# A new hand-written order for a fused sliding-window attention and gMLP kernel, with output stores as steps of their own

## The chip, the cores and the metric

One NeuronCore of a Trainium2 chip runs the whole computation. The metric is device time of one execution in microseconds, median over runs; smaller is better. TensorE is called PE in the profile's rows (PEld is its weight load), VectorE DVE, ScalarE ACT, GpSimd POOL and SyncE SP.

## What is computed

From one input x (2048 tokens by 512, bf16), normalised once, two branches are added to x: causal attention over a window of 256 keys with 32 heads of 16, and a gMLP whose spatial weight mixes all 2048 tokens.

```python
xn = _layernorm(x, axis=-1)
return x + _A_ref(xn, A_wqkv, A_wo) + _B_ref(xn, B_w_in, B_w_sp, B_b_sp, B_w_out)

# _A_ref: q, k, v from x @ wqkv, 32 heads of 16
mask = (idx[:, None] - idx[None, :] >= 0) & (idx[:, None] - idx[None, :] < W)   # W = 256
p = _softmax(jnp.where(mask[None, None], q @ k.T * Dh ** (-0.5), -1000000000.0), axis=-1)
out_A = (p @ v) @ wo

# _B_ref: F = 1376, Fh = 688
z = _gelu(x @ w_in)
z1 = z[..., :Fh].copy()
z2 = _layernorm(z[..., Fh:], axis=-1)
g = jnp.einsum('ts,bsf->btf', w_sp, z2) + b_sp[None, :, None]
out_B = (z1 * g) @ w_out
```

## The kernel before

The work is cut into small steps, each a Python function of a few instructions, and the order of all steps is written out by hand as three strings, STAGE1, STAGE2 and STAGE3 (lines 68 to 169), which `run` (L597) reads token by token. A token is a letter and its arguments. Every engine executes its instructions in the order in which they are emitted, so the strings set the order on each engine and on each DMA queue; semaphores only delay. A DMA that is issued on SP or POOL holds up the issues behind it in the same queue until what it waits for is there.

Tokens are split in 16 tiles of 128 (n below). The steps that the text speaks of:

- Stage 1, normalisation and the gMLP's first half. `a,n` takes statistics of x tile n on VectorE (L260), `A,lo,hi` makes 1/std of tiles lo to hi-1 on POOL in two instructions (L222), `b,n` normalises a tile on VectorE (L265; six buffers), `B,n` only centres tiles 0 to 2. `t`/`T` transpose a tile on TensorE and copy it, `d,n` transposes it by a DMA on SP (L297). `z,n,half,bank,p0,p1` multiplies a tile by half of w_in in two pairs of chunks (L304), `y,n,half,bank` applies gelu on ScalarE (L317). Of the second half `c,n` takes statistics on VectorE (L324), `C,lo,hi` makes 1/std on POOL, `e,n` normalises in place on VectorE (L330). `I,i` are set-up steps (L603): I,12 to I,19 load the attention's output weight, I,20 and I,21 the gMLP's, all as DMAs on POOL; I,8 clears regions on VectorE, I,9 one on POOL.
- Projections. For head group G (four of eight heads) and token block j (four of 512 tokens), `Q,G,j,bank,c0,c1` and `K,...` multiply chunks c0 to c1-1 into one of two PSUM banks, v or w (L337); `q,G,j,bank,engine` and `k,...` evict the bank on VectorE (D) or ScalarE (A) into a staging tile with two buffers; `F,G,j` and `G,G,j` spread it to its place by four to six, and four, DMAs of up to 64 KB (L357, L381), on SP for G = 0 and on POOL otherwise. `P,n`/`p,n` do the same for the values, without a spread.
- Attention. The window is laid out as a band of 4864 columns per head group, in ten pieces g. `S,G,g,e` (L425) writes 128 x 2048 scores into the only score tile, four PSUM banks; `X,G,g,e` (L436) is the exponential on ScalarE that empties it. So scores and exponentials alternate, 76 of each. `M,k` masks on VectorE, `V,i` (L489) multiplies by the values, `N,i,part` (L505) transposes and divides on VectorE.
- Mixing. `w,n` loads the transposed rows n of w_sp by a DMA on SP into one of three buffers (L530), `H,n,half,bank,c0,c1` multiplies chunks of it into bank v or w (L535), `h,n,half,bank` adds the bias and gates on VectorE. `u,n` transposes the result by a DMA on SP (L550); u,n overwrites what u,n-1 read.
- Output. `r,n` loads x tile n again by a DMA on POOL (L558) into one of two buffers, `O,n,bank,...` and `R,n,bank,...` multiply by the gMLP's and the attention's output weight into one bank, `o,n,bank` (L577) adds x on VectorE into one of two buffers and stores it by a DMA on SP.

Stage 2 runs attention, mixing and the first output tiles together; stage 3 has the last output tiles, for which four more PSUM banks (i, j, k, l) are free. The pool of the w_sp buffers is opened after stage 1's pools are closed (L684), and so may take their place.

Of the kernel before, what the change touches and what calls it, by code (L numbers as in the profile page):

```python
# [90 lines left out]
P,0,w,0,4 p,5,v,D M,0 S,0,1,1 I,13 P,1,v,0,4 p,0,w,D X,0,1,1 p,1,v,D P,2,w,0,4 M,1 P,11,v,0,1
w,1 p,2,w,A S,0,2,0 I,14 c,12 P,11,v,1,3 X,0,2,0 P,3,w,0,3 e,10 C,12,16 P,11,v,3,4 M,2 F,0,2 V,0
e,5 p,11,v,A S,0,2,1 I,15 e,15 P,3,w,3,4 X,0,2,1 P,8,v,0,4 p,3,w,D P,10,w,0,4 p,8,v,D G,0,2 M,3
Q,0,3,v,0,1 p,10,w,A S,0,3,0 I,16 e,6 Q,0,3,v,1,2 X,0,3,0 P,13,w,0,4 e,2 e,8 Q,0,3,v,2,3 e,14
V,1 M,4 p,13,w,A S,0,3,1 I,17 Q,0,3,v,3,4 X,0,3,1 P,12,w,0,4 q,0,3,v,D e,12 F,0,3 P,15,v,0,4
p,12,w,D p,15,v,A M,5 S,0,4,0 I,18 Q,1,0,w,0,1 X,0,4,0 P,4,v,0,4 w,2 Q,1,0,w,1,4 p,4,v,D N,0,0
q,1,0,w,A S,0,4,1 I,19 K,1,0,v,0,2 X,0,4,1 F,1,0 N,0,1 H,0,0,w,0,3 K,1,0,v,2,4 e,9 V,2 k,1,0,v,D
S,0,5,0 I,20 M,6 H,0,0,w,3,7 G,1,0 X,0,5,0 P,14,v,0,1 N,1,0 H,0,0,w,7,8 P,14,v,1,2 H,0,0,w,8,12
e,13 P,14,v,2,3 H,0,0,w,12,13 M,7 S,0,5,1 I,21 H,0,0,w,13,16 X,0,5,1 V,3 h,0,0,w N,1,1
H,0,1,w,0,5 M,8 S,0,6,0 H,0,1,w,5,9 X,0,6,0 M,9 P,14,v,3,4 H,0,1,w,9,16 p,14,v,D H,1,0,v,0,2  # L100
h,0,1,w S,0,6,1 N,2,0 H,1,0,v,2,3 u,0 K,1,1,w,0,1 X,0,6,1 H,1,0,v,3,5 K,1,1,w,1,2 H,1,0,v,5,6
K,1,1,w,2,4 w,3 k,1,1,w,D V,4 S,0,7,0 N,2,1 H,1,0,v,6,10 X,0,7,0 Q,1,1,w,0,1 M,10 H,1,0,v,10,16
Q,1,1,w,1,3 h,1,0,v S,0,7,1 M,11 Q,1,1,w,3,4 X,0,7,1 H,1,1,v,0,13 N,3,0 q,1,1,w,D M,12 S,0,8,0
F,1,1 H,1,1,v,13,16 X,0,8,0 H,2,0,w,0,11 h,1,1,v w,4 N,3,1 G,1,1 S,0,8,1 V,5 X,0,8,1 N,4,0
H,2,0,w,11,16 H,2,1,v,0,4 h,2,0,w S,0,9,0 M,13 H,2,1,v,4,6 X,0,9,0 Q,1,2,w,0,2 M,14 H,2,1,v,6,8
Q,1,2,w,2,3 N,4,1 H,2,1,v,8,9 V,6 S,1,0,0 Q,1,2,w,3,4 X,1,0,0 H,2,1,v,9,16 q,1,2,w,D H,3,0,w,0,6
h,2,1,v w,5 N,5,0 S,1,0,1 K,1,2,v,0,1 X,1,0,1 H,3,0,w,6,7 M,15 K,1,2,v,1,2 H,3,0,w,7,8
K,1,2,v,2,4 u,1 H,3,0,w,8,9 k,1,2,v,D V,7 M,0 S,1,1,0 H,3,0,w,9,16 X,1,1,0 N,5,1 H,3,1,v,0,7
# [613 lines left out]
```

## Time and profile before

| what | value |
|---|---|
| median of three runs | 266.68 us |
| the three runs | 264.35, 266.68, 269.54 us |
| the profiled execution, own time | 267.68 us |
| its span, first to last instruction | 266.0 us |
| granted TensorE clock, mean | 0.992 |
| busy TensorE, VectorE, ScalarE, POOL | 252.3, 187.1, 178.5, 90.1 us |
| 76 exponentials: busy, one | 142.6, 1.877 us |
| first and last exponential start | 49.91, 248.04 us |
| POOL's key copies: issue, landing (median) | 0.625, 4.5 us |
| SP's loads of w_sp: landing (median) | 5.2 us |

The profile is of one execution. A row of the timeline gives start, duration, engine and line, what is written from what, and in brackets how long the engine idled before and what ended that. A q behind an engine's name marks its queue of issues, where a duration can cover several issues (xcount). A row of windows gives a stretch, its length, and the busy time of each engine in it. TensorE's matmuls overlap, so that its busy time is an upper bound of its work.

### The profile page before, as it was taken

How to read it: one execution, taken by the hardware profiler on the slowest of the kernel's cores; microseconds unless marked ns; L12 is line 12 of the kernel's file. 1: busy time of each engine (PE TensorE's matmuls, PEld its weight loads, DVE VectorE, ACT ScalarE, POOL GpSimd, SP SyncE). 2: the span in 40 equal slices, each digit the busy share in tenths (PEclk: the TensorE clock that was granted, in tenths of full speed). 3: DMA queues.
4: the chain of work that ended last, by engine and by line, in shares of the span. 5: the costliest groups of instructions: out<-in, count | busy, mean ns of one | idle time of the engine just before them, and what ended most of it. 6: DMA issues, size and time to landing. Idle time of an engine off the chain costs nothing.

```text
span 266.0 us, 8993 instructions
## 1 busy us (share of the span) xinstructions
PE 252.3 (95%) x3876; PEld 140.4 (53%) x3916; DVE 187.1 (70%) x415; ACT 178.5 (67%) x137; POOL 90.1 (34%) x168
## 2 busy tenths in 40 slices
PE   7999999898999999999999979999989999999993
PEld 6565555343455566555555644565646544444541
DVE  4779977979688858476878654777467577666573
ACT  3675556788976867877778755867867786767300
POOL 6432230406080250197221923062163206511130
PEclk9999999999999999999999997999999999999999
DMA  6994243267474566779643872996396313422233
GB/s 196 364 266 99 55 93 70 49 142 172 78 174 125 100 141 111 99 175 212 123 91 79 167 127 62 108 148 121 74 172 130 70 32 111 131 81 83 81 98 99
DMA packets 69431, 32.65 MB, mean 123 GB/s; under 512 B 60288, under 2 KB 66528, under 8 KB 69392
## 3 DMA queue, kind: packets, MB, share of 16 engines
q1 hardware_dynamic: 64864, 22.50, 41.3%
q0 software_dynamic: 4496, 9.58, 15.4%
q8 instruction: 30, 0.49, 0.8%
q14 instruction: 9, 0.07, 0.1%
q10 hardware_dynamic: 32, 0.00, 0.0%
HBM read 8.41 MB, written 2.10 MB: 40 GB/s over the span
## 4 chain that ended last, share of the span: by engine, by line
PE 47%; DMA 13%; DVE 13%; issue 13%; POOL 8%; ACT 3%; SPq 1%; POOLq 0%; DVEq 0%; ACTq 0%
PE w L538 25%; PE w L339 7%; PE sS L429 6%; PE oP L501 5%; DMA x_ch<-in_A_x_dram 5%; DVE st L327 5%; PE w L394 3%; POOL q L366 3%; DMA wspT<-in_B_w_sp_dram 3%; DMA xs<-in_A_x_dram 2%; ACT E L443 2%; POOL kbd L387 2%; DMA kbd<-kz 2%; DVE st L262 2%; DVE xn L267 2%
## 5 line engine op out<-in xcount | busy, mean ns | idle before, releaser
L443 ACT ACTIVATE E<-sS 128x2048 bf16<-128x2048 f32 x76 | 142.6, 1877 | 50.7 <-PE sS L429 48.4
L538 PE MATMUL w<-z,wspT 128*128 128x344 bf16 x512 | 93.9, 314 | 1.9 <-DMA wspT<-in_B_w_sp_dram 1.1
L538 PEld LDWEIGHTS <-wspT 128*128 128x128 bf16 x512 | 47.1, 99 | 32.2 <-issue 5.6
L366 POOL DMA_DIRECT2D q<-qs x54 | 28.0, 527 | 73.5 <-DVE qs L355 36.8
L452 DVE TENSOR_TENSOR E<-E,mask 128x1024 bf16<-128x1024 bf16 x52 | 34.5, 672 | 4.8 <-ACT E L443 4.6
L339 PE MATMUL w<-xnT,wqkv 128*128 128x512 bf16 x105 | 34.8, 382 | 1.6 <-DVE v_all L405 0.8
L387 POOL DMA_DIRECT2D kbd<-kz x48 | 29.5, 625 | 13.6 <-DVE kz L379 8.9
L429 PE MATMUL sS<-q,kbd 32*128 32x320 bf16 (+4 forms) x816 | 30.5, 244 | 2.2 <-DMA kbd<-kz 1.8
L545 DVE SCALAR_TENSOR_TENSOR z1u<-w,b_all,z1u 128x344 bf16<-128x344 f32 x32 | 17.9, 560 | 17.7 <-PE w L538 17.6
L509 DVE STREAM_TRANSPOSE a<-oP 128x512 f32<-128x512 f32 x32 | 22.6, 705 | 9.2 <-PE oP L501 9.1
L501 PEld LDWEIGHTS <-v_all 64*17 64x17 bf16 x1920 | 22.3, 85 | 9.2 <-issue 9.0
L501 PE MATMUL oP<-E,v_all 64*17 64x256 bf16 (+3 forms) x1920 | 26.2, 230 | 0.0
L429 PEld LDWEIGHTS <-kbd 32*128 32x128 bf16 x816 | 12.5, 92 | 24.3 <-issue 22.6
L309 PEld LDWEIGHTS <-xnT 128*128 128x128 bf16 x208 | 18.1, 98 | 12.4
L560 POOL DMA_DIRECT2D x_ch<-in_A_x_dram x16 | 8.7, 545 | 38.4 <-DVE out_sb L579 32.7
L566 PE MATMUL w<-w_out_sb,z1u 128*128 128x512 bf16 x67 | 18.5, 381 | 0.6 <-DVE out_sb L579 0.4
L339 PEld LDWEIGHTS <-wqkv 128*128 128x128 bf16 x128 | 12.2, 98 | 12.2 <-issue 3.4
L394 PE MATMUL w<-wqkv,xnT 128*128 128x512 bf16 x61 | 15.7, 379 | 0.8 <-DVE v_all L405 0.3
L379 DVE CAST kz<-w 128x256 bf16<-128x256 f32 x28 | 10.5, 418 | 6.6 <-PE w L339 6.4
L522 DVE STREAM_TRANSPOSE oT<-b 128x256 bf16<-128x256 bf16 x32 | 14.2, 445 | 1.1
L327 DVE BATCH_NORM_STATS2 st<-z 128x6 f32<-128x344 bf16 x32 | 14.5, 496 | 0.0
L262 DVE BATCH_NORM_STATS2 st<-xs 128x6 f32<-128x512 bf16 x16 | 10.8, 677 | 4.6 <-DMA xs<-in_A_x_dram 4.6
(87 smaller groups left out, 246.4 us busy)
## 6 DMA issues: line engine op xcount, KB each, us to landing
kbd<-kz POOLq DMA_DIRECT2D x48, 64.0 KB, 4.5
q<-qs POOLq DMA_DIRECT2D x36, 64.0 KB, 3.0
x_ch<-in_A_x_dram POOLq DMA_DIRECT2D x16, 128.0 KB, 3.3
out_dram<-out_sb SPq DMA_DIRECT2D x16, 128.0 KB, 2.0
wqkv<-in_A_wqkv_dram SPq DMA_DIRECT2D x1, 1536.0 KB, 10.8
xs<-in_A_x_dram SPq DMA_DIRECT2D x2, 512.0 KB, 7.5
kbd<-kz SPq DMA_DIRECT2D x16, 64.0 KB, 2.1
q<-qs SPq DMA_DIRECT2D x14, 64.0 KB, 2.0
```

The source lines that it names most:

```text
L327: nc.vector.bn_stats(out=st[:, j, :], in_=z2[:, n, j * FQ : (j + 1) * FQ])
L339: nc.tensor.matmul(banks[bank], lhsT=wqkv[:, c, col : col + P], rhs=xnT[:, c, tok : tok + 512], start=(c == 0), stop=(c == NDC - 1),)
L366: eng.dma_start(out=q2[h : P : 2, e, c : c + w], in_=t[64 * e : 64 * e + 64, src0 + at : src0 + at + w],)
L387: eng.dma_start(out=kbd[h : P : 2, slot : slot + 4, e, :], in_=t[64 * e : 64 * e + 64, h, :].rearrange("p (k m) -> p k m", k=4),)
L394: nc.tensor.matmul(banks[bank], lhsT=xnT[:, c, n * P : (n + 1) * P], rhs=wqkv[:, c, 2 * D : 3 * D], start=(c == 0), stop=(c == NDC - 1),)
L429: nc.tensor.matmul(s_bank(s)[:, off + o : off + o + w], lhsT=kbd[32 * s : 32 * s + 32, slot, ee, :], rhs=q2[32 * s : 32 * s + 32, ee, c : ...
L443: nc.scalar.activation(out=dst, in_=src, func=ACT.Exp, scale=SM_SCALE)
L452: nc.vector.tensor_tensor(out=reg, in0=reg, in1=mask[:].rearrange("p a m -> p (a m)").unsqueeze(1).to_broadcast([P, 8, 128]), op=ALU.mult,)
L501: nc.tensor.matmul(skip_group_check=True, **args)
L509: nc.vector.transpose(out=a32[:].rearrange("p e c r -> p (e c r)"), in_=oP[i % 2][:])
L538: nc.tensor.matmul(banks[bank][:, 0:FQ], lhsT=w[:, c, :], rhs=z2[:, c, half * FQ : (half + 1) * FQ], start=(c == 0), stop=(c == NB - 1),)
L566: nc.tensor.matmul(banks[bank], lhsT=uT[:, c, :], rhs=w_out_sb[:, c, :], start=(c == 0), stop=False)
```

## The change

The three strings are written anew: nearly every step of the three stages changes place, the split of projections and mixing into chunks changes, and so do some banks and some evicting engines. The steps themselves and their number stay, with three differences. The output store is cut out of `o` and becomes a step `v,n`. The pool of the w_sp buffers is opened ahead of stage 1's pools, so that it has room of its own, and w,0 moves into stage 1. All loads of output weights (I,12 to I,21) move into the end of stage 1; before they stood in stage 2.

The diff, cut to the code and to the lines of the strings that the text speaks of:

```diff
 STAGE1 = """
...
-y,2,0,a z,4,1,b,0,2 b,2 y,3,0,o A,6,9 a,9 d,2 z,3,1,a,0,1 y,4,1,b z,5,1,o,0,2 b,6 A,9,10 a,10
-d,6 z,4,0,b,0,2 y,5,1,o b,7 A,10,11 b,8 d,7 a,11 z,5,0,o,0,2 y,4,0,b a,12 d,8 z,3,1,a,1,2
...
-z,6,1,b,0,2 c,3 d,10 z,7,1,o,0,1 y,6,1,b a,14 K,0,0,w,2,3 z,7,1,o,1,2 c,5 A,11,15 z,8,0,a,0,1
-y,7,1,o z,8,1,b,0,1 q,0,0,v,A b,11 z,9,1,o,0,2 b,12 d,11 b,13 c,6 z,8,1,b,1,2 d,13 K,0,0,w,3,4
...
-z,11,0,b,0,2 c,4 d,15 z,11,1,a,0,2 y,11,0,b c,0 F,0,0 z,14,0,b,0,2 y,11,1,a C,0,4 y,7,0,o C,4,8
-z,13,1,a,0,1 e,1 y,14,0,b c,9 G,0,0 K,0,1,v,3,4 z,12,1,o,0,1 z,13,1,a,1,2 c,8 z,12,1,o,1,2
...
-y,15,0,o c,13 z,10,0,b,0,1 y,14,1,a c,10 z,6,0,o,0,1 z,10,0,b,1,2 e,0 C,8,12 c,15 z,13,0,a,0,2
-y,10,0,b c,14 z,6,0,o,1,2 y,13,0,a z,12,0,b,0,2 y,6,0,o e,7 P,6,w,0,1 y,12,0,b
...
+b,0 y,2,0,b z,3,0,a,0,2 b,1 d,0 T,4,v,A a,7 y,2,1,o t,5,w z,3,1,b,0,2 a,8 d,1 T,5,w,A b,2 A,6,9
+z,4,0,o,0,2 y,3,1,b d,2 b,6 y,3,0,a z,5,0,b,0,1 b,7 d,6 y,4,0,o b,8 z,4,1,a,0,1 a,9 z,5,0,b,1,2
...
+b,10 a,12 K,0,0,w,3,4 d,10 y,6,0,a z,7,0,b,0,2 a,13 z,6,1,o,1,2 y,7,0,b a,14 z,8,1,a,0,1 y,6,1,o
+z,8,0,b,0,1 A,11,15 k,0,0,w,A z,8,1,a,1,2 b,11 z,8,0,b,1,2 y,8,1,a a,15 z,10,1,o,0,1 K,0,1,w,0,1
+b,12 z,7,1,a,0,2 c,2 d,12 z,10,1,o,1,2 y,7,1,a c,0 d,11 Q,0,0,v,3,4 K,0,1,w,1,3 y,8,0,b
+z,10,0,a,0,2 b,13 C,0,4 y,10,1,o c,8 d,13 A,15,16 z,12,1,b,0,2 y,10,0,a c,5 z,11,1,o,0,2
...
+z,11,0,o,0,1 y,13,1,b z,9,0,a,0,1 q,0,0,v,A c,6 z,11,0,o,1,2 d,15 I,9 z,14,1,b,0,1 y,11,0,o I,12
+c,13 z,9,0,a,1,2 w,0 z,9,1,o,0,1 y,9,0,a I,13 c,4 z,14,1,b,1,2 z,14,0,a,0,1 y,14,1,b I,14 c,12
+C,4,8 F,0,0 K,0,1,w,3,4 z,9,1,o,1,2 c,14 z,15,1,b,0,1 y,9,1,o I,15 z,14,0,a,1,2 k,0,1,w,A e,3
+z,15,1,b,1,2 e,2 y,14,0,a I,16 e,7 z,15,0,o,0,2 G,0,1 c,9 y,15,1,b I,17 z,12,0,a,0,2 y,15,0,o
+I,18 e,5 C,8,12 Q,0,1,v,0,1 y,12,0,a I,19 I,20 I,21
 """
 
 STAGE2 = """
-P,6,w,1,3 Q,0,1,v,0,1 P,6,w,3,4 J,1 Q,0,1,v,1,4 p,6,w,D S,0,0,0 q,0,1,v,D K,0,2,w,0,4 X,0,0,0
...
-H,8,0,w,5,6 M,13 K,2,2,v,1,4 u,5 H,8,0,w,6,7 k,2,2,v,D V,14 N,13,0 G,2,2 S,2,0,0 H,8,0,w,7,16
-X,2,0,0 M,14 M,15 H,8,1,v,0,5 N,13,1 F,2,2 u,6 S,2,0,1 H,8,1,v,5,14 X,2,0,1 h,8,0,w V,15 G,2,1
...
-X,2,7,1 Q,3,1,w,0,1 H,13,0,v,6,9 M,10 Q,3,1,w,1,2 w,14 H,13,0,v,9,10 M,11 Q,3,1,w,2,4
...
+P,6,w,0,1 e,8 Q,0,1,v,1,4 e,0 J,1 P,6,w,1,2 q,0,1,v,D S,0,0,0 P,6,w,2,4 F,0,1 K,0,3,v,0,4
...
+S,1,8,0 N,11,1 V,13 X,1,8,0 F,2,2 H,7,0,w,10,16 H,7,1,v,0,3 h,7,0,w S,1,8,1 N,12,0 H,7,1,v,3,16
+X,1,8,1 N,12,1 G,2,1 M,12 H,8,0,w,0,1 w,10 S,1,9,0 M,13 H,8,0,w,1,5 X,1,9,0 h,7,1,v F,2,1 V,14
...
+H,12,0,w,0,2 h,11,1,v w,14 S,2,6,0 M,8 H,12,0,w,2,6 X,2,6,0 K,3,1,v,0,2 M,9 H,12,0,w,6,7
...
+O,9,w,4,5 R,8,v,2,3 O,9,w,5,6 S,3,8,1 R,8,v,3,4 X,3,8,1 R,9,w,0,4 o,8,v r,10 O,11,v,0,6 o,9,w
+v,9 r,11 M,13 u,15 R,11,v,0,2 S,3,9,0 V,30 X,3,9,0
 """
 
 STAGE3 = """
...
-R,15,l,1,4 R,14,k,0,4 o,15,l o,14,k
+v,8 N,29,0 O,10,w,0,6 N,29,1 R,11,v,2,3 R,10,w,0,1 O,14,i,0,1 M,14 O,12,j,0,1 O,13,k,0,1
...
+R,13,k,0,1 N,30,1 R,12,j,0,1 O,15,l,1,2 R,13,k,1,3 O,15,l,2,4 R,13,k,3,4 R,12,j,1,4 o,13,k V,32
+o,12,j v,13 r,15 O,15,l,4,5 N,31,0 v,12 r,14 O,14,i,1,2 O,15,l,5,6 O,14,i,2,3 R,15,l,0,2 N,31,1
+O,14,i,3,4 R,15,l,2,3 O,14,i,4,6 R,15,l,3,4 R,14,i,0,4 o,15,l v,15 o,14,i v,14
 """
...
+    wsp_pool = ctx.enter_context(tc.tile_pool(name="wsp_pool", bufs=3))
+
 
     stage1 = ExitStack()
...
     x_tiles = {}
+    out_tiles = {}
...
     def keep_out(n, bank):
         out_sb = cpool.tile([P, D], BF, name="out_sb")
+        out_tiles[n] = out_sb
         nc.vector.tensor_tensor(
             out=out_sb[:], in0=banks[bank], in1=x_tiles.pop(n)[:], op=ALU.add
         )
-        nc.sync.dma_start(out=out2[n * P : (n + 1) * P, :], in_=out_sb[:])
+
+    def store_out(n):
+        nc.sync.dma_start(out=out2[n * P : (n + 1) * P, :], in_=out_tiles.pop(n)[:])
...
-        "H": mix, "h": keep_mix, "u": transpose_u, "O": out_u, "R": out_o, "o": keep_out,
+        "H": mix, "h": keep_mix, "u": transpose_u, "O": out_u, "R": out_o, "o": keep_out, "v": store_out,
...
     cpool = ctx.enter_context(tc.tile_pool(name="cpool", bufs=2))
-    wsp_pool = ctx.enter_context(tc.tile_pool(name="wsp_pool", bufs=3))
     run(STAGE2)
```

More of the change, by code (lines that the diff above doesn't have):

```diff
@@ L91 @@
[L91 to L108, printed above, removed]
@@ L157 @@
[L157 to L159 removed]
+P,6,w,0,1 e,8 Q,0,1,v,1,4 e,0 J,1 P,6,w,1,2 q,0,1,v,D S,0,0,0 P,6,w,2,4 F,0,1 K,0,3,v,0,4
+p,6,w,D X,0,0,0 P,7,w,0,4 k,0,3,v,D c,15 K,0,2,v,0,1 p,7,w,A S,0,0,1 w,1 K,0,2,v,1,4 X,0,0,1
+C,12,16 P,9,w,0,4 k,0,2,v,D r,1 e,1 Q,0,2,v,0,2 p,9,w,A m S,0,1,0 Q,0,2,v,2,4 X,0,1,0 P,0,w,0,4
@@ new lines @@
+K,1,0,w,1,2 X,0,4,1 F,1,0 H,0,0,v,0,4 e,13 K,1,0,w,2,3 e,12 H,0,0,v,4,5 K,1,0,w,3,4 e,10 V,2
+N,0,1 S,0,5,0 H,0,0,v,5,12 k,1,0,w,D X,0,5,0 N,1,0 G,1,0 P,14,w,0,2 H,0,0,v,12,16 h,0,0,v
+S,0,5,1 P,14,w,2,3 M,7 X,0,5,1 H,0,1,v,0,3 P,14,w,3,4 H,0,1,v,3,6 p,14,w,D V,3 M,8 S,0,6,0
+H,0,1,v,6,16 X,0,6,0 N,1,1 H,1,0,w,0,4 h,0,1,v w,3 M,9 S,0,6,1 H,1,0,w,4,6 X,0,6,1 N,2,0
+K,1,1,v,0,1 H,1,0,w,6,7 K,1,1,v,1,4 u,0 k,1,1,v,D V,4 S,0,7,0 M,10 G,1,1 H,1,0,w,7,8 Q,1,1,v,0,2
+X,0,7,0 H,1,0,w,8,12 Q,1,1,v,2,3 H,1,0,w,12,13 Q,1,1,v,3,4 H,1,0,w,13,15 q,1,1,v,D S,0,7,1
@@ new lines @@
+H,1,0,w,15,16 F,1,1 H,1,1,v,0,8 X,0,7,1 h,1,0,w N,2,1 Q,1,2,w,0,1 H,1,1,v,8,12 M,11 S,0,8,0
+N,3,0 Q,1,2,w,1,2 X,0,8,0 H,1,1,v,12,16 Q,1,2,w,2,3 h,1,1,v w,4 V,5 N,3,1 H,2,0,v,0,1 S,0,8,1
+M,12 H,2,0,v,1,9 X,0,8,1 N,4,0 Q,1,2,w,3,4 H,2,0,v,9,14 q,1,2,w,D M,13 S,0,9,0 F,1,2
+H,2,0,v,14,16 X,0,9,0 H,2,1,w,0,1 N,4,1 V,6 h,2,0,v H,2,1,w,1,5 N,5,0 K,1,2,v,0,1 S,1,0,0
+H,2,1,w,5,7 X,1,0,0 M,14 K,1,2,v,1,2 H,2,1,w,7,10 M,15 K,1,2,v,2,3 H,2,1,w,10,14 K,1,2,v,3,4
+H,2,1,w,14,15 k,1,2,v,D S,1,0,1 V,7 X,1,0,1 H,2,1,w,15,16 H,3,0,v,0,8 h,2,1,w w,5 N,5,1 S,1,1,0
@@ new lines @@
+H,5,1,w,0,3 N,9,0 K,2,0,v,0,1 H,5,1,w,3,5 S,1,5,0 M,7 K,2,0,v,1,2 X,1,5,0 H,5,1,w,5,6
+K,2,0,v,2,3 N,9,1 H,5,1,w,6,11 K,2,0,v,3,4 H,5,1,w,11,15 k,2,0,v,D u,2 S,1,5,1 H,5,1,w,15,16
+G,2,0 H,6,0,v,0,5 X,1,5,1 h,5,1,w w,8 K,2,1,w,0,1 H,6,0,v,5,6 V,11 N,10,0 S,1,6,0 K,2,1,w,1,4
+X,1,6,0 H,6,0,v,6,16 k,2,1,w,D M,8 S,1,6,1 M,9 H,6,1,w,0,9 X,1,6,1 h,6,0,v V,12 S,1,7,0
+H,6,1,w,9,16 X,1,7,0 Q,2,1,v,0,4 h,6,1,w w,9 M,10 H,7,0,w,0,2 q,2,1,v,A S,1,7,1 N,10,1
+H,7,0,w,2,3 Q,2,2,v,0,2 X,1,7,1 H,7,0,w,3,7 M,11 u,3 Q,2,2,v,2,4 N,11,0 H,7,0,w,7,10 q,2,2,v,A
@@ new lines @@
+u,5 H,9,0,v,9,13 Q,2,3,w,3,4 H,9,0,v,13,15 q,2,3,w,D V,16 F,2,3 S,2,2,0 N,15,0 H,9,0,v,15,16
+H,9,1,w,0,14 X,2,2,0 h,9,0,v M,2 S,2,2,1 H,9,1,w,14,16 X,2,2,1 H,10,0,v,0,6 h,9,1,w w,12 N,15,1
+K,2,3,w,0,1 H,10,0,v,6,11 M,3 S,2,3,0 K,2,3,w,1,2 X,2,3,0 H,10,0,v,11,13 K,2,3,w,2,3
+H,10,0,v,13,14 K,2,3,w,3,4 H,10,0,v,14,16 k,2,3,w,D V,17 h,10,0,v G,2,3 S,2,3,1 H,10,1,w,0,4
+N,16,0 X,2,3,1 Q,3,0,v,0,2 H,10,1,w,4,12 M,4 M,5 S,2,4,0 H,10,1,w,12,16 X,2,4,0 V,18 h,10,1,w
+w,13 N,16,1 Q,3,0,v,2,3 H,11,0,w,0,3 M,6 S,2,4,1 Q,3,0,v,3,4 X,2,4,1 H,11,0,w,3,16 u,6 q,3,0,v,D
@@ new lines @@
+Q,3,1,w,3,4 H,13,0,v,8,10 q,3,1,w,D S,2,8,0 V,21 M,12 F,3,1 X,2,8,0 u,8 N,20,0 H,13,0,v,10,16
+H,13,1,w,0,4 h,13,0,v G,3,1 S,2,8,1 N,20,1 K,3,2,v,0,1 X,2,8,1 H,13,1,w,4,7 K,3,2,v,1,2
+H,13,1,w,7,8 K,3,2,v,2,3 H,13,1,w,8,10 K,3,2,v,3,4 H,13,1,w,10,13 k,3,2,v,D S,2,9,0
+H,13,1,w,13,16 M,13 X,2,9,0 u,9 H,14,0,v,0,6 M,14 V,22 h,13,1,w M,15 S,3,0,0 Q,3,2,w,0,1 X,3,0,0
+H,14,0,v,6,7 N,21,0 Q,3,2,w,1,2 H,14,0,v,7,9 Q,3,2,w,2,3 H,14,0,v,9,16 u,10 N,21,1 h,14,0,v
+S,3,0,1 V,23 X,3,0,1 N,22,0 H,14,1,v,0,2 Q,3,2,w,3,4 H,14,1,v,2,8 u,11 q,3,2,w,A M,0 S,3,1,0
@@ new lines @@
+H,14,1,v,8,16 X,3,1,0 F,3,2 M,1 H,15,0,w,0,7 h,14,1,v N,22,1 G,3,2 S,3,1,1 V,24 X,3,1,1 u,12
+H,15,0,w,7,16 h,15,0,w S,3,2,0 Q,3,3,v,0,1 X,3,2,0 N,23,0 H,15,1,w,0,3 Q,3,3,v,1,2 H,15,1,w,3,4
+Q,3,3,v,2,4 M,2 u,13 H,15,1,w,4,8 q,3,3,v,D S,3,2,1 N,23,1 H,15,1,w,8,9 K,3,3,v,0,1 X,3,2,1
+H,15,1,w,9,13 M,3 K,3,3,v,1,2 H,15,1,w,13,14 K,3,3,v,2,4 H,15,1,w,14,16 k,3,3,v,D S,3,3,0 V,25
+h,15,1,w X,3,3,0 G,3,3 M,4 O,0,v,0,2 O,1,w,0,1 O,0,v,2,4 N,24,0 O,1,w,1,3 S,3,3,1 N,24,1
+O,1,w,3,5 X,3,3,1 O,0,v,4,6 R,0,v,0,3 O,1,w,5,6 R,0,v,3,4 R,1,w,0,1 o,0,v S,3,4,0 R,1,w,1,4
```

100 lines of the change are left out of this document (37 added, 63 removed).

## The prediction

> **What bounds the kernel now.** I read the page's busy shares first, then the start times of the exponentials, then the windows and the timeline at each place where their spacing breaks, last the chain of waits.
>
> ```profile
> PE 252.3 (95%) x3876; PEld 140.4 (53%) x3916; DVE 187.1 (70%) x415; ACT 178.5 (67%) x137; POOL 90.1 (34%) x168
> ...
> PEclk9999999999999999999999997999999999999999
> ```
>
> TensorE is the bound, but busy time covers stretched matmuls, so I count its work instead, by start-to-start times in undisturbed stretches: 0.215 us for a 512-column matmul (fourteen tail matmuls from 250.20 to 253.22), 0.154 for a mixing matmul (fourteen in 2.15), 0.585 for two gating chunks, 0.33 for a score step, 0.75 for a visit. Summed over every token of either order this is 243.4 us; the change alters no matmul. "Position" below is this running sum. Real start less position is the loss so far: 6.4 us at the first exponential (49.91), 7.4 at the second, 9.6 at S,0,6,0, 10.9 just before S,2,2,0, 14.7 two exponentials on, 15.0 before S,3,0,0, 16.4 at it, 18.3 at the last. Only stalls can be won, and these are the large ones.
>
> ```profile
> 152.24 2.47 POOL L387 DMA_DIRECT2D kbd<-kz  x4
> ...
> 158.75 0.29 PE L429 MATMUL sS<-q,kbd 32*128 32x256 bf16 x4 [1.83 <-DMA kbd<-kz]
> ...
> 159.09 1.88 ACT L443 ACTIVATE E<-sS 128x2048 bf16<-128x2048 f32 x1 [2.56 <-PE sS L429]
> ...
> 163.42 1.88 ACT L443 ACTIVATE E<-sS 128x2048 bf16<-128x2048 f32 x1 [2.45 <-PE sS L429]
> ```
>
> Scores S,2,2,0 wait for keys G,2,1, issued on POOL behind G,2,2 and F,2,2. The windows show that the stall costs twice: after it the clock is down.
>
> ```profile
> 156.90:158.75 1.85, 0.02 (x5) 0.03 (x1) 0.75 (x2) 0.00 (x0) 0.00 (x0) 1.00 0.69 127
> 158.75:162.90 4.15, 4.15 (x18) 1.86 (x18) 0.69 (x1) 1.88 (x1) 0.34 (x1) 0.59 0.00 0
> ```
>
> The columns are busy time of PE, PEld, DVE, ACT and POOL, then the granted clock: 0.59 in the second row. The loss grows by 2.07 and 1.72 between exponentials: 3.8 us from one late transfer. The second stall is a mixing weight tile (w,14) that SP issued late, behind four z1u transposes:
>
> ```profile
> 190.78 6.67 SPq L532 DMA_TRANSPOSE wspT<-in_B_w_sp_dram  x2
> ...
> 198.07 1.05 PE L538 MATMUL w<-z,wspT 128*128 128x344 bf16 x6 [1.08 <-DMA wspT<-in_B_w_sp_dram]
> ```
>
> It adds 1.35 to the loss. The third place is where stage 1 meets stage 2: TensorE waits for an eviction on a VectorE that runs late.
>
> ```profile
> 49.86 0.69 DVE L405 CAST v_all<-w 128x512 bf16<-128x512 f32 x1
> 50.46 0.68 DVE L355 CAST qs<-w 128x512 bf16<-128x512 f32 x1
> ...
> 50.60 2.25 PE L339 MATMUL w<-xnT,wqkv 128*128 128x512 bf16 x9 [0.84 <-DVE v_all L405]
> ```
>
> VectorE is behind because of waits in stage 1, three of which the reader needs:
>
> ```profile
> 18.88 0.41 DVE L267 TENSOR_SCALAR xn<-xs,mvx,rstdx 128x512 bf16<-128x512 bf16 x1 [1.45 <-DMA xnT<-xn]
> ...
> 27.12 1.06 DVE L267 TENSOR_SCALAR xn<-xs,mvx,rstdx 128x512 bf16<-128x512 bf16 x3 [0.42 <-POOL rstdx L227]
> ...
> 37.65 0.46 DVE L331 TENSOR_SCALAR z<-z,mv,rstd 128x688 bf16<-128x688 bf16 x1 [1.48 <-POOL rstd L227]
> ```
>
> **The change part by part.**
>
> Keys G,2,1 and weight tile w,14. G,2,1 stood 4.9 us of TensorE work ahead of its first reader; it now stands 12.9 ahead. From POOL's issue to landing these copies took 2.1 to 6.4 us and an issue is 0.62, so four issues plus the slowest landing, 8.3, fit. Gain 3.8. w,14 stood 6.6 ahead, now 15.9; its kind landed in 4.2 to 9.4. Gain 1.35. What is late next: of all key and query spreads of stage 2, the shortest distances are now F,2,1 (6.6, was 13.0) and F,3,3 (6.8, was 5.1 without a stall). The other w stand 14 or more ahead.
>
> F,2,1. On POOL's queue it comes behind F,2,2 (six issues, 3.4 with the pauses between them) and G,2,1 (four, 2.5). F,2,2 waits for the eviction of Q,2,2, at position 129.2, so F,2,1's four issues (2.1) end near 137.1, the last begins near 136.5, and S,2,1,0 is at 140.9. 4.4 us are left; POOL's query copies landed in 1.6 to 6.6, median 3.0. By the median there is no stall, and I take 0; by the slowest 2.2 us, and a clock drop of 1.7 on top: ends 0 and 3.9. Behind the waiting F,2,2 are G,2,1 and F,2,1 only.
>
> [...]
>
> Stage 1's new order on VectorE. Its work up to the eviction of q,0,1 is the same: 39.5 us of instructions, against 39.4 before p,6 in the old order. Its waits are not. (a) b,6, b,7 and b,8 now follow b,2 with nothing between, while before a,9 and a,10 (0.82 each) lay in the wait of 1.45; b,5 stands ahead of a,6: together about 1.2 more. (b) b,11 follows POOL's A,11,15 directly; before, the statistics c,5 (1.08) lay between and 0.42 was left: 1.06 more. (c) e,8 follows C,8,12 with one 0.4 us normalisation between; that POOL pair took 1.48 in the row at 37.65: 1.1 more. (d) That row's own wait goes, since c,14, e,3 and e,2 now cover C,4,8: 1.48 less. Sum 1.9. So q,0,1 is evicted from about 51.9 to 52.5 and the projection K,0,3 starts near 52.6 where the old one started at 50.60: loss 2.0. Ends: -0.8 (VectorE on time, so that the 0.84 wait goes too) and +3.7 (2.0 with a clock drop, 1.7). I take 2.0, because each wait has its row. On the way z,12 can wait 0.8 for its transposed tile (d,12 now 2.4 us ahead, was 4.9); this lies inside the same lateness, since TensorE then waits less at the boundary.
>
> On the clock: here an idle of 1.83 us was followed by the low clock, one of 1.08 at 198 was not. The boundary's idle would be about 2 us, so a drop is possible; I leave it out of the sum as it stands between these two and hangs on the estimate. [...]
>
> Values, projections and evictions (from S,0,0,1 to S,0,6,0) lost 2.2 us before. Twelve bank reuses closer than 1 us stand there in both orders, six of the value evictions on ScalarE in both. I take 0, ends -1 and +1. Later evictions on ScalarE go from five to four; one lengthened an exponential's interval by 0.2 at most (111.71 less 109.06, against 2.5): 0.
>
> Output weights in stage 1 (I,12 to I,21). Ten POOL issues (0.52 to 0.93 each, 6.2 us) move ahead of C,4,8, C,8,12 and C,12,16. POOL is idle there (busy 3.21 of 20 us from 40 to 60), and the issues wait for nothing, so they are through before the statistics they precede; first use is past position 200. r,1 goes from position 107 to 48 on the same queue; it waits for nothing, and o,1 reads it past 205. Cost 0; without that cover each issue ahead of C,8,12 would cost 0.6.
>
> Weight pool ahead of stage 1's: w,0 now goes out on SP between d,15 and F,0,0. Its issue took 2.1; F,0,0 (four issues, 2.5, landing 2.0) is at position 36.9 and first read at 43.1, so 6.2 against 4.5 if F follows at once. First mixing matmul at 65.2 in both orders. Cost 0, end +0.4.
>
> The store as a token of its own. Same sixteen DMAs, 0.33 us of SP each. Queued behind v,9 is u,15: issued near 230.0, landing 2.7 to 5.8 (median 3.8), read at 234.7. By the median 0, end +1.1. v,8 follows u,15, so o,11, which reuses its buffer, can slip under 1 us, with nothing on TensorE behind it.
>
> Tail. r,15 waited for o,13, r,14 for o,12; now o,12's last matmul is 0.4 later and r,15 itself waits for o,12, so r,14 issues 0.7 later. Its landing sets the end now:
>
> ```profile
> 258.29 1.13 POOL L560 DMA_DIRECT2D x_ch<-in_A_x_dram  x2 [3.49 <-DVE out_sb L579]
> 262.26 0.69 DVE L579 TENSOR_TENSOR out_sb<-tk,x_ch 128x512 bf16<-128x512 f32 x1 [0.47 <-DMA x_ch<-in_A_x_dram]
> ```
>
> Cost 0.7, ends 0.2 and 1.5.
>
> Sum against the profiled execution, 267.68 (span 266.0 and 1.68 around it): 267.68 - 3.8 - 1.35 + 2.0 + 0.7 = 265.2. That execution stands 1.0 above the median of the three runs, 266.68, which lie 5.2 apart.
>
> **The rivals.**
> 1. The boundary costs nothing: VectorE is in time. For it: identical work up to there. Against: the waits (a) to (c). 267.68 - 5.15 - 0.8 + 0.7 = 262.4, and 261.4 if the value phase gains 1.
> 2. A new stall at S,2,1,0 takes the place of the old at S,2,2,0: POOL's queue again, F,2,1 behind F,2,2 and G,2,1. It decides when F,2,1 lands more than 4.4 us after its last issue. For it: copies next to w transposes took 5.5 to 6.6 at 191.8 and w,10 goes out just there; against: 1.8 to 3.8 at 149 to 152. 265.2 + 3.9 = 269.1: slower than before.
> 3. The order does not cure the late transfers, as landing times grow with traffic and not with place: the 5.15 stays, 265.2 + 5.15 = 270.4. Against: distances of 12.9 and 15.9.
> 4. Small waits I do not see, in an order moved throughout, one with a clock drop among them (1.83 + 1.7): 268.7 to 273.
>
> **How the numbers follow.** Forecast 0.42 (own range 263.3 to 267.2), rival 1 0.2, rival 2 0.18, rival 3 0.06, rival 4 0.14. The range 261.4 to 270.4 takes in the first three and leaves out about 2 in 10: the far end of rival 4, rivals 2 or 3 with a second drop, and rival 1 with more gained. A measurement here tells about 2% from no change: faster is under 261.3 (half of rival 1, 0.1), slower over 272.0 (most of rival 4, a part of 2 and 3: 0.14), the rest 0.76.
>
> **What would show it.** Right: no TensorE wait for kbd before S,2,2,0, the granted clock full from 150 to 165, no wait for wspT near S,3,0,0. The boundary: the first projection after S,0,0,0 starts at 52 or later, VectorE idle before b,11 and e,8; if it starts by 50.6, rival 1. A TensorE wait for q at S,2,1,0 is rival 2. The last x_ch lands some 0.7 later, counted from the last exponential. Wrong altogether if stalls over 1.8 us stand elsewhere.

## The result

The changed kernel takes 268.32 us (median of 22 runs, 267.14 to 269.26). The kernel before, run beside it, takes 268.5 (22 runs, 264.14 to 276.07), so the plain medians are the same within 0.1%. The ratio of the two is 1.0078, 95% interval 1.0054 to 1.0102; like the ratios of the experiments, it leaves out executions more than 1.5% above the fastest of their kernel, which are 12 of the 22 of the kernel before and none of the changed kernel's. By this ratio the change makes the kernel about 0.8% slower; 265.2, some 0.9% faster than the profiled execution before, was forecast. The profiled execution after has a span of 267.2 (1.2 more than before) and is at the upper end of its 22 spans (265.1 to 267.3).

On the page after, TensorE's busy time has risen by 4.4 us with the same matmuls (the trace before lacks the records of 40 of them), and the dip of the granted clock has moved from the 25th slice to the ninth:

```profile
PE 256.7 (96%) x3916; PEld 139.4 (52%) x3916; DVE 188.2 (70%) x415; ACT 178.8 (67%) x137; POOL 89.6 (34%) x168
...
PEclk9999999979999999999999999999999999999998
```

The two stalls that were to go are gone. ScalarE's timeline around the former key stall (exponentials X,2,2,0 and X,2,2,1, once 159.09 and 163.42, each after 2.5 us of waiting):

```profile
162.52 1.88 ACT L447 ACTIVATE E<-sS 128x2048 bf16<-128x2048 f32 x1 [0.62 <-PE sS L433]
165.21 1.88 ACT L447 ACTIVATE E<-sS 128x2048 bf16<-128x2048 f32 x1 [0.81 <-PE sS L433]
```

They now follow each other after 2.69 us instead of 4.33. The windows there have the full clock (1.00, the first number after POOL's):

```profile
158.00:163.00 5.00, 5.00 (x92) 2.86 (x90) 2.96 (x6) 3.63 (x3) 1.93 (x4) 1.00 0.93 139
```

And the mixing matmuls with tile w,14 have no wait ahead of them (this row holds the last three with w,13 and the first six with w,14):

```profile
198.32 1.49 PE L542 MATMUL w<-z,wspT 128*128 128x344 bf16 x9
```

The loss is where stage 1 meets stage 2. VectorE's timeline:

```profile
19.76 1.15 DVE L271 TENSOR_SCALAR xn<-xs,mvx,rstdx 128x512 bf16<-128x512 bf16 x3 [2.79 <-DMA xnT<-xn]
...
30.07 0.41 DVE L271 TENSOR_SCALAR xn<-xs,mvx,rstdx 128x512 bf16<-128x512 bf16 x1 [1.49 <-POOL rstdx L229]
...
52.06 0.83 DVE L335 TENSOR_SCALAR z<-z,mv,rstd 128x688 bf16<-128x688 bf16 x2 [1.24 <-POOL rstd L229]
52.80 0.69 DVE L359 CAST qs<-w 128x512 bf16<-128x512 f32 x1
```

These are the three waits that the prediction named, (a) at b,6, (b) at b,11 and (c) at e,8, and the eviction of q,0,1 that e,8 holds up. TensorE's timeline shows what the late eviction does:

```profile
50.35 0.60 PE L398 MATMUL w<-wqkv,xnT 128*128 128x512 bf16 x2
53.54 1.71 PE L343 MATMUL w<-xnT,wqkv 128*128 128x512 bf16 x4 [2.58 <-DVE qs L359]
...
57.26 0.40 PE L433 MATMUL sS<-q,kbd 32*128 32x320 bf16 x8
```

TensorE idles 2.58 us (0.84 before) and then needs 1.71 us for four matmuls that take 1.02 where the clock is 1.00 (a_xnp10 below, at 51.29). The windows of idle time and what follows:

```profile
50.95:53.54 2.59, 0.01 (x2) 0.00 (x1) 1.48 (x4) 1.91 (x2) 2.56 (x4) 1.00 0.22 39
53.54:57.26 3.72, 3.72 (x10) 1.13 (x10) 2.35 (x6) 0.27 (x1) 0.55 (x2) 0.54 0.70 200
```

The clock falls to 0.54 for 3.7 us. The scores S,0,0,1 start at 57.26; before, it was 52.78. Real starts of exponentials show where each kernel stands; the names at the top are those of the experiments below.

| exponential | before | after | a_wout_late | a_q_first_wout_late | hybrid | b_late_cured | b_cured_xnp10 |
|---|---|---|---|---|---|---|---|
| X,0,0,0 | 49.91 | 51.00 | 50.61 | 50.48 | 49.97 | 49.95 | 49.49 |
| X,0,1,0 | 55.69 | 60.23 | 59.78 | 56.35 | 55.59 | 55.73 | 54.38 |
| X,1,1,0 | 104.18 | 108.31 | 107.85 | 104.43 | 104.18 | 104.21 | 102.88 |
| X,1,6,1 | 132.03 | 135.84 | 135.38 | 131.96 | 131.67 | 132.06 | 130.73 |
| X,2,1,1 | 154.65 | 160.03 | 159.47 | 156.08 | 155.57 | 155.66 | 153.35 |
| X,2,2,1 | 163.42 | 165.21 | 164.65 | 161.26 | 160.75 | 160.78 | 158.46 |
| X,3,0,1 | 202.93 | 204.03 | 203.46 | 199.97 | 199.37 | 199.04 | 196.68 |
| X,3,9,0 | 248.04 | 249.59 | 248.55 | 245.76 | 244.55 | 243.88 | 242.24 |
| span | 266.0 | 267.2 | 267.3 | 263.4 | 262.3 | 261.8 | 260.3 |

After less before: +4.54 at X,0,1,0, +3.81 at X,1,6,1, +5.38 at X,2,1,1, +1.79 at X,2,2,1, +1.88 at X,2,9,0, +1.10 at X,3,0,1, +1.55 at the last, and 1.2 in the span. So 3.6 and 0.8 us are won at the two stalls, 4.5 at the boundary and another 1.6 between 135 and 160 are lost, and the rest is small differences either way (0.7 won back before 135).

### The profile page after: what moved, and what is told of

The parts are those of the page before. It is cut to its first block, busy times and chain, and to the rows that moved or that the text cites. A ratio compares the mean times of both kernels' runs of the same rounds, so it can differ in the third digit from the quotient of the medians.

```text
span 267.2 us, 9037 instructions
## 1 busy us (share of the span) xinstructions
PE 256.7 (96%) x3916; PEld 139.4 (52%) x3916; DVE 188.2 (70%) x415; ACT 178.8 (67%) x137; POOL 89.6 (34%) x168
## 4 chain that ended last, share of the span: by engine, by line
PE 40%; issue 20%; DVE 13%; POOL 12%; DMA 10%; ACT 1%; SPq 1%; POOLq 0%; DVEq 0%; ACTq 0%
PE w L542 13%; PE w L571 5%; PE w L343 5%; PE sS L433 5%; POOL kbd L391 5%; POOL q L370 5%; PE w L398 5%; DVE st L331 4%; PE oP L505 4%; PE w L577 3%; DMA q<-qs 2%; DMA x_ch<-in_A_x_dram 2%; DMA xs<-in_A_x_dram 2%; DVE st L266 2%; DMA xnT<-xn 2%
## 5 line engine op out<-in xcount | busy, mean ns | idle before, releaser
L343 PE MATMUL w<-xnT,wqkv 128*128 128x512 bf16 x128 | 42.6, 388 | 2.6 <-DVE qs L359 2.6
L398 PE MATMUL w<-wqkv,xnT 128*128 128x512 bf16 x64 | 17.7, 396 | 0.0
L313 PE MATMUL za<-w_in_sb,xnT 128*128 128x512 bf16 x80 | 14.1, 309 | 0.0
```

The lines of the kernel that those rows point to most:

```text
L313: nc.tensor.matmul(zp[:, lo:hi], lhsT=xcT[:, n, c, :] if n < NCEN else xnT[:, c, n * P : (n + 1) * P], rhs=w_in_sb[:, c, f0 + lo : f0 + hi ...
L343: nc.tensor.matmul(banks[bank], lhsT=wqkv[:, c, col : col + P], rhs=xnT[:, c, tok : tok + 512], start=(c == 0), stop=(c == NDC - 1),)
L398: nc.tensor.matmul(banks[bank], lhsT=xnT[:, c, n * P : (n + 1) * P], rhs=wqkv[:, c, 2 * D : 3 * D], start=(c == 0), stop=(c == NDC - 1),)
```

## The experiments

Theory A: VectorE's lateness at the end of stage 1 makes the boundary's loss, by the idle and by the clock after it. Theory B: the output weights' loads, now beside the queries' transfers F,0,1, make it. Ratios are to the kernel before, run alternately on the same chip, with 95% intervals.

**a_q_first: two normalisations behind the eviction.**

```diff
-P,6,w,0,1 e,8 Q,0,1,v,1,4 e,0 J,1 P,6,w,1,2 q,0,1,v,D S,0,0,0 ... p,6,w,D X,0,0,0
+P,6,w,0,1 Q,0,1,v,1,4 J,1 P,6,w,1,2 q,0,1,v,D S,0,0,0 ... p,6,w,D e,8 e,0 X,0,0,0
```

> The changed kernel with the two normalisations e,8 and e,0 moved behind the evictions of q,0,1 and p,6 on VectorE. Theory A (VectorE's lateness at the end of stage 1 makes the loss; the change's kernel has q,0,1 evicted at 52.80, TensorE idle 2.58 us in front of K,0,3 and half the clock for 3.4 us after): q,0,1 is evicted near 50.6, the idle falls to 1 us or less, the clock stays full, S,0,0,1 starts near 53.5 instead of 57.26, and the span falls by 3 to 3.8 us, to some 263.5 to 264.2. Theory B (the output weights' transfers, now beside those of q,0,1, hold up F,0,1's landing and so the next steps): S,0,1,0 still waits for F,0,1, which lands 5 us after issue, and the span falls by 1 us or less.

Span 264.5, ratio 0.9987 (0.9941 to 1.0034). The exponential X,0,0,1 starts at 53.43 instead of 57.71. TensorE's timeline:

```profile
50.53 1.02 PE L339 MATMUL w<-xnT,wqkv 128*128 128x512 bf16 x4 [0.52 <-DVE qs L355]
...
56.38 0.35 PE L429 MATMUL sS<-q,kbd 32*128 32x320 bf16 x8 [0.65 <-DMA q<-qs]
```

The idle is 0.52, and the four matmuls take 1.02 us, as at the full clock, instead of 1.71, as theory A has it. But S,0,1,0 now waits for F,0,1's queries: a part of B is true as well, behind A.

**a_filler: eight matmuls of no use in the idle,** written to an output bank that is cleared later.

```diff
-P,6,w,2,4 F,0,1 K,0,3,v,0,4
+P,6,w,2,4 F,0,1 D,8 K,0,3,v,0,4
```

> The changed kernel with eight 512-column matmuls of no use (into an output bank that is set to zero later) put in front of K,0,3, where TensorE idles 2.58 us; VectorE's times stay as they are. They take 1.7 us of the idle and leave 0.9. If the half clock after it (3.4 us from 53.7) is caused by the idle, it goes away, S,0,0,1 starts at 55.5 instead of 57.26, and the time falls by about 1.7 us (theory A: 2.6 idle plus 1.7 clock). If the low clock has another cause, or if the transfers of F,0,1 set the pace (theory B), the time stays within 0.3.

Span 267.9, ratio 1.0046 (1.0005 to 1.0088): nothing gained. The clock stays full (1.00 from 53.35 to 57.00) and X,0,0,1 starts 1.73 us earlier, as expected of the clock, and then TensorE gives it back:

```profile
53.35 1.02 PE L339 MATMUL w<-xnT,wqkv 128*128 128x512 bf16 x3 [0.74 <-DVE qs L355]
...
59.56 0.35 PE L429 MATMUL sS<-q,kbd 32*128 32x320 bf16 x8 [1.28 <-DMA q<-qs]
```

X,0,1,0 is only 0.27 earlier than in the changed kernel. The half clock was not alone: F,0,1's landing would have cost nearly the same at the same time.

**a_wout_late: output weights back into stage 2,** one load behind each of ten score steps.

```diff
-y,11,0,o I,12 ... y,12,0,a I,19 I,20 I,21
+S,0,1,0 I,12 ... S,0,1,1 I,13 ... S,0,5,1 I,21
```

> The changed kernel with the ten loads of the output weights (I,12 to I,21) moved back into stage 2, one behind each of ten score steps from S,0,1,0 on. Theory A: no change of the boundary, S,0,0,1 at 57 still, time within 0.4 of the changed kernel. Theory B: F,0,1 lands in 2 us instead of 5.2, the boundary loses 1 to 2 us less and the time falls by that.

Span 267.3, ratio 1.0017 (0.9963 to 1.007). F,0,1's four transfers, in the trace's answer for the query tile (issue, then time to landing), first in the changed kernel:

```profile
L370 SPq DMA_DIRECT2D q<-qs x4: 484/594/596, 53.5 to 55.3; - x4
...
DMA to landing us min/median/max: 4.3/5.2/5.2
```

and with the loads back in stage 2:

```profile
L366 SPq DMA_DIRECT2D q<-qs x4: 485/595/624, 53.1 to 54.9; - x4
...
DMA to landing us min/median/max: 1.9/2.1/2.5
```

The landing is cured, by 3 us, and X,0,1,0 comes 0.45 earlier only, because TensorE still idles 2.58 and has a clock of 0.55 after it. So in the changed kernel two limits stand side by side, each of which hides the other: the half clock, and the slow landing. The spans of this kernel's executions fit that, though a mean clock does not say where the drop fell: with 0.997 or more they are 263.6 and 264.3, with 0.995 or 0.996 265.5 to 266.7, with 0.991 or less 265.8 to 267.3. In the changed kernel, where the slow landing stands beside the clock, the clock hardly shows: its eight executions with a mean clock of 1.000 have a median span of 266.3, the nine under 0.995 one of 266.8.

**b_late_cured and b_late_cured_2: the old order with two transfers moved alone.**

```diff
-V,15 G,2,1 ... Q,3,1,w,1,2 w,14
+F,2,1 G,2,1 ... h,11,1,w w,14
```

> The kernel before with two transfers alone moved: G,2,1 goes to just behind F,2,1 (14 us of TensorE work ahead of its first reader instead of 4.9) and w,14 to just behind h,11,1. Theory A, by which the changed kernel won both stalls and lost as much at the boundary: the stall and the low clock at 158 and the stall at 198 go, 3.8 + 1.35 = 5.1 us, so about 261 to 262.5 in span. Rival C (the stalls move elsewhere, because other late transfers follow at once): 1 to 3 us are gained.

> The old order with G,2,1 and w,14 issued early once more, in five rounds, to have the ratio of the two moved transfers with a narrower interval: 0.984 to 0.988 by the first run's span (261.8 against 266.0) and times.

Spans 261.8 and 261.7, ratios 0.9847 (0.9771 to 0.9924) and 0.9893 (0.9849 to 0.9937). The former stall, on ScalarE's timeline of the first:

```profile
158.10 1.88 ACT L439 ACTIVATE E<-sS 128x2048 bf16<-128x2048 f32 x1 [0.56 <-PE sS L425]
160.78 1.88 ACT L439 ACTIVATE E<-sS 128x2048 bf16<-128x2048 f32 x1 [0.80 <-PE sS L425]
```

From X,2,1,1 to X,3,0,1 it gains 4.9 us on the kernel before, and it loses 1.0 up to X,1,8,1, most of it in one wait (last section). Rival C, stalls that move on, is refuted: what the changed order was to win can be had by two moved tokens.

**a_filler_wout_late and a_q_first_wout_late: both limits taken away, in two ways** (the edits above, joined).

> The changed kernel with both the eight filler matmuls in front of K,0,3 and the output weights' loads moved back into stage 2. In the run with the filler alone S,0,0,1 came 1.73 us earlier, but S,0,1,0 then waited 1.28 us for F,0,1's queries, which took 5 us to land beside the output weights. Theory: VectorE's lateness is the first limit at the boundary and the slow landing a second one behind it; with both taken away the queries land in 2 us, S,0,1,0 waits for nothing, and 1.3 to 1.7 us that the clock drop cost are kept: span about 265.6 to 266. Rival: the landing is slow for another reason (the transposing load of w,0 just behind it), and the span stays at 267.3 or above.

> The changed kernel with e,8 and e,0 behind the evictions of q,0,1 and p,6, and the output weights' loads moved back into stage 2: the boundary with both limits taken away. Theory: S,0,0,1 at 53.4 as in the run with the first edit alone, S,0,1,0 without its wait of 0.65 us for F,0,1, so that the loss at X,0,1,0 falls from 7.9 to about 7.2, and the span by another 0.6 us, to some 263.9. Rival: the loads spread over stage 2 collide there with the queries and keys and cost what they free at the boundary: span 264.5 or above.

With filler: span 265.4, ratio 1.0007 (0.9967 to 1.0047); X,0,1,0 starts at 57.80, 2.16 earlier than with the filler alone, with no wait for queries. The clock's share can thus be won, once the landing is fast. The transposing load behind F,0,1 (w,1; the expectation calls it w,0) stands there as before, as it does in a_wout_late, where F,0,1 lands in 2.1 us, so it is not what slowed the landing. With the evictions first: span 263.4, ratio 0.9939 (0.9901 to 0.9976), S,0,1,0 waits for nothing, X,0,1,0 at 56.35 instead of 56.78. So the loads cost 0.4 us in the changed kernel and in a_q_first, and 2.2 where the filler keeps the clock full.

**a_xnp10: ten buffers instead of six for the normalised x.**

```diff
-xnp = stage1.enter_context(tc.tile_pool(name="xnp", bufs=6))
+xnp = stage1.enter_context(tc.tile_pool(name="xnp", bufs=10))
```

> The changed kernel with ten instead of six buffers for the normalised x (xnp), nothing else. b,6 waits 2.79 us on VectorE, until d,0 has landed at 19.66, though its scale factors are ready at 18.0. Theory A: the wait is one for a buffer, b,6 starts near 18.1, VectorE is 1.6 us earlier from there to the end of stage 1, q,0,1 is evicted near 51.2, TensorE's idle at K,0,3 falls from 2.58 to about 1.0, the clock stays full, S,0,0,1 starts near 54; then F,0,1's landing (5 us) is the limit, and 2 us in all are gained. Rival: VectorE's lead is eaten by its later waits for POOL (b,11, e,8), whose work starts when it does otherwise: q,0,1 at 52.5, gain 0.3 or less.

Span 263.9, ratio 1.0025 (0.9968 to 1.0081); the profiled execution is the lowest of ten spans, whose median is 264.7. The wait at b,6 on VectorE is now one for POOL, and 1.7 shorter:

```profile
17.61 1.06 DVE L267 TENSOR_SCALAR xn<-xs,mvx,rstdx 128x512 bf16<-128x512 bf16 x3 [1.10 <-POOL rstdx L225]
```

So it was a wait for a buffer. At the boundary the lead is still there (q,0,1 at 50.55, less 2.25), the idle is 1.8 us and the clock stays full. The windows:

```profile
49.50:51.29 1.79, 0.00 (x0) 0.00 (x0) 1.48 (x4) 1.79 (x2) 1.79 (x4) 1.00 0.15 37
51.29:55.00 3.71, 3.55 (x22) 1.50 (x23) 2.70 (x8) 1.74 (x3) 1.15 (x3) 1.00 0.67 197
```

**hybrid: the old order up to X,1,1,0, the changed one from there,** banks v and w exchanged in the second part. The work done at the cut is the same but for F,1,2, N,5,1, r,1 and u,1.

> The order before up to X,1,1,0 (stage 1, the boundary, output weights in stage 2, w,0 where it was), from there on the changed order with the bank names v and w exchanged. At the cut both orders have done the same work but for three issues. Theory A: the changed order's loss is the boundary's alone; the loss at X,1,1,0 is 8.6 instead of 12.7, the later starts are the changed kernel's less 4.1, and the span is 263.1 to 264.1 (tail 17.6 to 18.6). If it comes out at 262 or less, the changed order costs nothing more after the cut than the old one with its two late transfers cured (261.8); if 264 or more, it has losses of its own there, 1 us near 143 to 153 above all.

Span 262.3 (ten spans, 262.2 to 264.0, median 263.2), ratio 0.9912 (0.9873 to 0.9952). Without the changed boundary the changed order is faster than the old one. It stands 0.1 ahead of b_late_cured at X,2,1,1 and 0.7 behind at the last exponential: after the cut the new order is no better than the old one with two tokens moved.

**a_all: all three mendings of the changed kernel's boundary** (a_q_first, a_wout_late, a_xnp10).

> The changed kernel with its boundary mended in three ways: ten xnp buffers, e,8 and e,0 behind the evictions of q,0,1 and p,6, output weights in stage 2. With the last two the span was 263.4, with waits of 0.50 and 0.25 us left at the boundary; the buffers take 1.6 us of VectorE's lateness away, so both go: 262.5 to 262.9. That is still 0.7 to 1.1 above the old order with its two late transfers cured, since the changed order keeps small waits near 143 and 153. If the buffers bring nothing here, 263.4.

Span 263.0 (twelve spans, median 262.5), ratio 0.9928 (0.9896 to 0.996). X,0,1,0 starts at 55.67, 0.7 earlier than without the buffers: what was lost at the boundary is back. The one wait left there is 0.38 for an eviction.

**b_wout_early: the old order with the output weights alone in stage 1.**

```diff
-S,0,1,0 I,12 ... S,0,1,1 I,13 ... S,0,5,1 I,21
+y,7,0,o I,12 ... y,14,1,a I,18 ... y,12,0,b I,19 I,20 I,21
```

> The old kernel with the ten loads of the output weights alone put into stage 1, behind the same numbers of gelus from its end as in the changed order (I,18 ahead of C,8,12, the last three at the end). The prediction gave this step 0: span 266.0. If the loads slow the landing of F,0,1 from 2 to 5 us, as in the changed kernel, S,0,1,0 (old start of its exponential 55.69) waits for the queries, which are issued from 51.1 to 53.2 on: it starts near 57.5 to 58, and the span rises by 1.5 to 2.3 us.

Ratio 0.9990 (0.9948 to 1.0032), span 262.8. The expectation fell: X,0,1,0 starts at 56.12, 0.43 later than before. The last loads are issued at 49.3 and 50.2 here, the queries F,0,1 from 51.6 on, and these land in 2.1 to 3.3 us. In the changed kernel I,19 to I,21 stand behind C,8,12, which waits for VectorE, and so go out at 52 to 53.5, together with F,0,1. So here the early loads did little harm, and loads at the same moment as the queries did. The low span has two other reasons. One is in the windows at the key stall, which this kernel still has:

```profile
157.35:159.20 1.85, 0.02 (x4) 0.03 (x1) 0.74 (x2) 0.00 (x0) 0.00 (x0) 1.00 0.73 172
159.20:163.00 3.80, 3.80 (x33) 2.18 (x34) 1.15 (x2) 2.66 (x2) 0.93 (x2) 1.00 0.00 0
```

The same idle of 1.83 as before, and no clock drop after it (0.59 then): 1.65 less between X,2,1,1 and X,2,2,1. The other is w,14, which was not moved here: the second stall does not show (X,3,0,0 follows X,2,9,0 after 2.55 us instead of 3.82), and X,3,0,0 comes another 1.26 earlier. So neither the clock's share of the first stall nor the second stall is there in every execution of the old order.

**b_cured_xnp10: the old order, two tokens moved, ten buffers.**

> The old order with G,2,1 and w,14 issued early, and ten instead of six buffers for the normalised x. In the old order b,6 waits 1.45 us on VectorE for a buffer, until d,0 has landed, and TensorE waits 0.84 us at the boundary for VectorE. By the theory that VectorE's lateness at the end of stage 1 is made of such waits, b,6 starts 0.5 to 1 us earlier, the 0.84 at the boundary shrinks by as much, and the span falls from 261.8 to 261.0 to 261.3. Rival: a later wait for POOL takes the lead away, span 261.8.

Span 260.3, 262.29 us (median of six, 261.78 to 263.19), ratio 0.9848 (0.981 to 0.9887): the lowest of all kernels here. Beside it on the same chip, b_late_cured_2 takes 263.63 and the kernel before 267.29. On VectorE b,6 starts at 17.09 after 0.28, and S,0,0,1 on TensorE follows without a wait:

```profile
51.47 0.40 PE L425 MATMUL sS<-q,kbd 32*128 32x320 bf16 x8
```

X,0,1,0 starts at 54.38, 1.3 earlier than in the kernel before, and the median is 1.3 under b_late_cured_2's. The larger lead over b_late_cured at X,2,1,1 (2.3) is in part chance: the wait near 142 us (last section) is absent in this profile.

## Why the prediction was wrong

The two cured stalls and VectorE's lateness were the mechanisms of the working; the sum failed at the boundary. For the span it had -2.4 us, and the profiles show +1.2. Of the difference 2.5 is the boundary, 1.6 lies between 135 and 160 us, 0.8 are the two stalls, which gave 4.4 instead of 5.15; the tail gives 1.0 back, and the rest is small.

- Keys G,2,1: 3.8 forecast, 3.6 measured in the changed kernel and in b_late_cured. Right, for this base. About 2.0 of it is the late transfer itself (b_late_cured against b_wout_early, from X,2,1,1 to X,2,2,1), and 1.65 the clock, which differs from execution to execution: the stall of 1.83 was followed by the low clock in the profiled execution before (0.59) and not in b_wout_early's (1.00). Of the 48 executions of the kernel before that the experiments' ratios use, the 22 with a mean clock of 0.999 or more have a median span of 264.45, the 18 under 0.995 one of 265.75. The base of the sum, 267.68 with a span of 266.0, had a drop in it, which the sum counts as won.
- w,14: 1.35 forecast, 0.8 measured in the changed kernel and 1.3 in b_late_cured. The wait went, as forecast; in b_wout_early's execution it did not occur even with w,14 in its old place.
- The boundary, "So q,0,1 is evicted from about 51.9 to 52.5 and the projection K,0,3 starts near 52.6 where the old one started at 50.60: loss 2.0." This step failed: K,0,3 starts at 53.54, and X,0,1,0 4.54 later than before. Of the excess over 2.0, 0.9 is VectorE, most of it (a): a new wait of 0.47 at b,5 and 1.34 more at b,6 (2.79 less 1.45) make 1.81, not 1.2. The wait at b,6 was one for a buffer, which ends when d,0 has landed (b,6 starts at 19.76, once at 18.88); the prediction sized it by the statistics a,9 and a,10 that no longer stood in it, of which a,10 came behind b,6 in the old order too. (b) was 1.07 (1.49 less 0.42), as forecast, (c) 1.24 for 1.1, and (d) went as forecast. The rest of the excess, 1.6, is what comes after the idle. "I leave it out of the sum" was said of the clock drop; the idle of about 2 in the forecast and the 2.58 measured both lie above the 1.83 that the low clock (0.59) had followed in the kernel before, not between that and 1.08, so it belonged in. The upper end, +3.7, had it; the measured 4.5 is beyond even that. In executions without the drop the span is hardly shorter (266.3 against 266.8 above), because of the next point.
- "Output weights in stage 1 ... Cost 0" failed too, hidden by the first. The prediction has it that "the issues wait for nothing"; but three of them stand behind C,8,12 on POOL, whose wait for VectorE (0.84 us, to 50.59) sends them out at 51.99 to 53.50, with F,0,1, which then lands in 5.2 us instead of 2.0. In a_filler, with the clock intact, that alone took 1.28 us back. Of the cause the runs show the landing times of F,0,1 alone: 5.2 us with the loads beside it, 2.1 with the loads in stage 2 (a_wout_late), 2.1 to 3.3 with the last of them just ahead (b_wout_early).
- Rival 2 (S,2,1,0 waits for F,2,1) came in a small form: waits for q of 0.40 to 0.81 us in three of the variants (a_q_first, a_xnp10, a_wout_late); in the changed kernel no such wait is shown, but X,2,1,0 comes 0.4 later against the kernel before than X,2,0,1.
- Rival 4, small waits: 1.1 us between X,1,6,1 and X,2,0,1, 0.51 of it a TensorE wait for which the profile shows no releaser (last section).
- Value phase 0: right (4.54 at X,0,1,0, 4.43 at X,0,6,0). Stores and u,15: 0.25 between X,3,7,0 and X,3,9,0, within the end given. Tail: 0.7 forecast, -0.35 measured in this execution (span less last exponential, 17.61 against 17.96), and -0.4 to 0.8 in the other kernels with the same tail, by when the last x tiles land. VectorE's last additions in the changed kernel and in a_q_first:

```profile
263.53 0.69 DVE L585 TENSOR_TENSOR out_sb<-ti,x_ch 128x512 bf16<-128x512 f32 x1 [0.35 <-DMA x_ch<-in_A_x_dram]
```

```profile
260.24 0.69 DVE L581 TENSOR_TENSOR out_sb<-tl,x_ch 128x512 bf16<-128x512 f32 x1 [1.94 <-DMA x_ch<-in_A_x_dram]
```

w,0 and its pool in stage 1 were not tried alone.

## What to carry to other kernels

Where a wait is cured by a new order, look at what moved up behind the engine that now runs latest; here two tokens moved in the old order gave what the whole new order was to give, and a larger pool of buffers gave 1.3 us more. A wait on a DMA in front of a write may be a buffer that is not free yet (2.79 us at b,6 with six buffers, 1.10 with ten): compare it with the time when the data were ready, and try a larger pool first. Two limits that end at the same moment hide each other, so an experiment that takes one away and gains nothing has not cleared it; take both away before calling either free.
